# A decode kernel with cached attention and an MLP: 256 KB cache slots become 512 KB units, wider score matmuls, 16 heads kept on chip

## Chip, cores, metric

One core of one Trainium2 chip. The time is the device time of one launch in microseconds, as the median of several runs; before and after always ran on the same chip in the same rounds.

## The reference

Two layers share their weights and caches (the code is shortened). Each layer adds attention over the last 1024 of 4096 cached tokens (32 heads of 128, 8 batch elements, one query each), then an MLP:

```python
def _A_ref(x, k_cache, v_cache, wq, wo):        # x 8x1x640, caches 8x32x4096x128
    W = min(4096, max(256, Sk // 4))            # 1024
    q = (x @ wq).reshape(B, 1, 32, 128).transpose(0, 2, 1, 3)
    k, v = k_cache[:, :, Sk - W:, :], v_cache[:, :, Sk - W:, :]
    p = softmax(einsum("bhqd,bhkd->bhqk", q, k) * Dh ** -0.5)
    return einsum("bhqk,bhkd->bhqd", p, v)....reshape(B, 1, 4096) @ wo
def _B_ref(x, w1, b1, w2, b2):                  # 640 -> 1728 -> 640
    return gelu(_layernorm(x) @ w1 + b1) @ w2 + b2
x = x + _A_ref(_layernorm(x), ...)   # layer 1
x = x + _B_ref(_layernorm(x), ...)
x = x + _A_ref(_layernorm(x), ...)   # layer 2: the same caches
x = x + _B_ref(_layernorm(x), ...)
```

One layer reads 134 MB of caches, so keeping heads on chip from the first layer for the second saves traffic. The inputs are drawn with a spread of 0.05.

## The kernel before

A slot is 128 partitions x 2 KB: one head's K or V, 1024 tokens, 8 tokens to a partition. Of 41 slots some hold loads in flight, some the 14 heads that are kept from a batch element's first layer for its second. A K slot is turned by VectorE (32x32 blocks) into a second slot, and small matmuls with N=4 give the scores.

```python
NSLOT = 41; NKEEP = 14; GH = 8; KT_RESERVE = 3; NSTREAM = H - NKEEP
...
def load(job, which, h):
    s = take()
    cache = A_k_cache if which == "k" else A_v_cache
    nc.sync.dma_start(slots[s][:],
                      cache[job.b, h, SK - W:, :].rearrange("(m c) d -> m (c d)", c=NC8))
...
def s_head(job, hi):
    ...
        nc.vector.transpose(slots[kt]..., slots[kn]...)      # (cut) 128x512 words
        free.append(kn)
    for g in range(2):
        for j in range(2):
            for e in range(2):
                o = 512 * j + 256 * g + e
                nc.tensor.matmul(job.s_ps[:, hi, g, :], lhsT=k[:, o:o + 255:2],
                                 rhs=qd[:, h, 2 * j + e, :], ...)
    if job.kind != "keep":
        free.append(job.kt.pop(h))
...
def softmax(job):    # (cut) exp; 16 matmuls turn p_s; a copy; 8 matmuls with ones for the sums
def o_head(job, hi): # (cut) 8 matmuls, N=1, V as the weights; then the slot is freed
def chain(b):        # (cut) MLP of layer 1, layer norm, q of layer 2: short dependent steps
...
for b in range(NB):
    drain(run_jobs(jobs))                        # layer 1 of b
    ch = chain(b)
    ...
    merge(run_jobs(again), ch, 2)                # layer 2 of b-1 beside the chain of b
    drain(run_jobs(keep(b, 1)))                  # layer 2 of b, kept heads
```

The softmax here doesn't subtract the row's maximum and nothing guards it: scores larger than these inputs give would overflow.

Of the kernel before, what the change touches and what calls it, by code (L numbers as in the profile page):

```python
# [28 lines left out]
NC8 = W // P  # L29

NSLOT = 41
NKEEP = 14
GH = 8
KT_RESERVE = 3
NSTREAM = H - NKEEP

# [5 lines left out]
def _chunks(lo, hi, step):  # L42
    return [list(range(h, min(h + step, hi))) for h in range(lo, hi, step)]

class Job:

    def __init__(self, b, layer, heads, kind):
        self.b, self.layer, self.heads, self.kind = b, layer, heads, kind
        self.kn, self.kt, self.vn = {}, {}, {}

@with_exitstack
def _kernel(ctx: ExitStack, tc: tile.TileContext, A_x, A_k_cache, A_v_cache, A_wq, A_wo,
            B_x, B_w1, B_b1, B_w2, B_b2, out):
    nc = tc.nc

# [5 lines left out]
    slotp = ctx.enter_context(tc.tile_pool(name="slots", bufs=1))  # L61
# [3 lines left out]
    psP = ctx.enter_context(tc.tile_pool(name="psP", bufs=1, space=bass.MemoryType.PSUM))  # L65
# [6 lines left out]
    ones_bf = const.tile([P, P], BF16, name="ones_bf")  # L72
    nc.vector.memset(ones_bf[:], 1.0)
# [9 lines left out]
    for j in range(2):  # L83
        for e in range(2):
            o = 64 * j + e
            nc.vector.tensor_copy(sel[:, 2 * j + e, :].rearrange("p (i r) -> p i r", i=4),
                                  ident[:, None, o:o + 63:2].to_broadcast([P, 4, 32]))

# [6 lines left out]

    slots = [slotp.tile([P, NC8 * DH], BF16, name=f"slot{i}") for i in range(NSLOT)]

    x_bf0 = slots[NSLOT - 1][0:NB, 0:D]
    nc.sync.dma_start(x_bf0, x_in[:, :])
    b1_row = slots[NSLOT - 2][0:NFC, 0:P]  # L100
    nc.gpsimd.memset(b1_row, 0.0)
    b2_row = slots[NSLOT - 2][0:NKC, P:2 * P]
# [27 lines left out]
    qd1 = state.tile([P, H, 4, 4], BF16, name="qd1")  # L130
    qd2 = [state.tile([P, H, 4, 4], BF16, name=f"qd2_{i}") for i in range(2)]

    free = list(range(NSLOT))

    def take():
        return free.pop(0)

    def layernorm(x, nb, dst, twice):
# [26 lines left out]
        yield  # L165

    def mlp(xv, xbv, nb, dst):
# [5 lines left out]
        for fc in range(NFC):  # L173
            for kc in range(NKC):
                nc.tensor.matmul(h_ps[:, fc, :], lhsT=w1_sb[:, kc, fc * P:(fc + 1) * P],  # L175
                                 rhs=yT[:, kc, :], start=(kc == 0), stop=(kc == NKC - 1))
        hx = small.tile([P, NFC, nb], FP32, tag=f"hx{nb}", name="hx", bufs=2 if nb == 1 else 1)
        nc.vector.tensor_tensor(out=hx[:], in0=h_ps[:],
                                in1=b1T[:, :, None].to_broadcast([P, NFC, nb]), op=ALU.add)
        u = small.tile([P, NFC, nb], FP32, tag=f"hu{nb}", name="hu", bufs=2 if nb == 1 else 1)  # L180
# [4 lines left out]
        th = small.tile([P, NFC, nb], FP32, tag=f"th{nb}", name="th", bufs=2 if nb == 1 else 1)  # L185
# [3 lines left out]
                                       op0=ALU.add, op1=ALU.mult)  # L189
        yield  # L190
        o_ps = psC.tile([P, NKC, nb], FP32, tag="c", name="o2_ps")
        for n in range(NKC):
            for fc in range(NFC):
                nc.tensor.matmul(o_ps[:, n, :], lhsT=w2_sb[:, fc, n * P:(n + 1) * P],  # L194
                                 rhs=g2[:, fc, :], start=(fc == 0), stop=(fc == NFC - 1))
        nc.vector.scalar_tensor_tensor(out=dst, in0=o_ps[:], scalar=0.5, in1=xbv,
                                       op0=ALU.mult, op1=ALU.add)

    def expand(qT, qd):
        e_ps = psC.tile([P, 4, H], FP32, tag="c", name="e_ps")  # L200
        for j in range(2):
            for e in range(2):
                nc.tensor.matmul(e_ps[:, 2 * j + e, :], lhsT=sel[:, 2 * j + e, :], rhs=qT,  # L203
                                 start=True, stop=True)
        nc.vector.tensor_tensor(  # L205
            out=qd[:],
            in0=e_ps[:].rearrange("p j h -> p h j")[:, :, :, None].to_broadcast([P, H, 4, 4]),
            in1=mask4[:, None, None, :].to_broadcast([P, H, 4, 4]), op=ALU.mult)

    def load(job, which, h):  # L210
        s = take()
        cache = A_k_cache if which == "k" else A_v_cache
        nc.sync.dma_start(slots[s][:],
                          cache[job.b, h, SK - W:, :].rearrange("(m c) d -> m (c d)", c=NC8))
        (job.kn if which == "k" else job.vn)[h] = s

    def s_head(job, hi):
        h = job.heads[hi]
        qd = qd1 if job.layer == 0 else qd2[job.b % 2]
        if hi == 0:  # L220
            job.s_ps = psS.tile([P, GH, 2, 4], FP32, tag="s_ps", name="s_ps")
        if h not in job.kt:
            kn, kt = job.kn.pop(h), take()
            nc.vector.transpose(  # L224
                slots[kt][:].bitcast(U32).rearrange("p (j gt c) -> p j gt c", j=2, c=32),
                slots[kn][:].bitcast(U32).rearrange("p (gt j r) -> p j gt r", j=2, r=32))
            free.append(kn)
            job.kt[h] = kt
        k = slots[job.kt[h]]
        for g in range(2):  # L230
            for j in range(2):
                for e in range(2):
                    o = 512 * j + 256 * g + e
                    nc.tensor.matmul(job.s_ps[:, hi, g, :], lhsT=k[:, o:o + 255:2],  # L234
                                     rhs=qd[:, h, 2 * j + e, :],
                                     start=(j == 0 and e == 0), stop=(j == 1 and e == 1))
        if job.kind != "keep":
            free.append(job.kt.pop(h))

    def softmax(job):  # L240
        n = len(job.heads)
        p_s = small.tile([P, GH, 2, 4], BF16, tag="p_s", name="p_s")
        nc.scalar.activation(p_s[:, 0:n], job.s_ps[:, 0:n], ACT.Exp, scale=QSCALE)  # L243
        p_ps = psP.tile([P, 4, GH * 2], FP32, tag="p_ps", name="p_ps")
        for t in range(4):
            for i in range(4):
                nc.tensor.matmul(p_ps[32 * i:32 * i + 32, t, 0:2 * n],  # L247
                                 lhsT=ident[:, 32 * t:32 * t + 32],
                                 rhs=p_s[:, 0:n, :, i].rearrange("p h g -> p (h g)"), start=True, stop=True)
        job.p_v = small.tile([P, 4, GH, 2], BF16, tag="p_v", name="p_v")  # L250
        nc.vector.tensor_copy(job.p_v[:, :, 0:n, :],  # L251
                              p_ps[:, :, 0:2 * n].rearrange("p t (h g) -> p t h g", g=2))
        job.o_ps = psO.tile([P, 2, GH], FP32, tag="o_ps", name="o_ps")
        for c in range(NC8):
            nc.tensor.matmul(job.o_ps[:, 1, 0:n], lhsT=ones_bf[:], rhs=job.p_v[:, c % 4, 0:n, c // 4],  # L255
                             start=(c == 0), stop=(c == NC8 - 1))

    def o_head(job, hi):
        h = job.heads[hi]
        v = slots[job.vn[h]]  # L260
        for c in range(NC8):
            nc.tensor.matmul(job.o_ps[:, 0, hi:hi + 1], lhsT=v[:, c * DH:(c + 1) * DH],  # L262
                             rhs=job.p_v[:, c % 4, hi, c // 4:c // 4 + 1],
                             start=(c == 0), stop=(c == NC8 - 1))
        if job.kind != "keep" or job.layer == 1:
            free.append(job.vn.pop(h))
        if job.layer == 1 and job.kind == "keep":
            free.append(job.kt.pop(h))

    def finish(job):  # L270
        n = len(job.heads)
        rd = small.tile([P, GH], FP32, tag="rd", name="rd")
        nc.vector.reciprocal(rd[:, 0:n], job.o_ps[:, 1, 0:n])  # L273
        if job.layer == 0:
            job.ot = small.tile([P, GH], BF16, tag="ot", name="ot")
            dst = job.ot[:, 0:n]
        else:
            dst = ot2[:, job.heads[0]:job.heads[0] + n, job.b]
        nc.vector.tensor_tensor(out=dst, in0=job.o_ps[:, 0, 0:n], in1=rd[:, 0:n], op=ALU.mult)  # L279

    att = {}

    def project(job):
        if job.heads[0] == 0:
            att[job.b] = psA.tile([P, NKC], FP32, tag="att", name="att")
        for hi, h in enumerate(job.heads):
# [5 lines left out]
    def stream(b, layer):  # L292
        return [Job(b, layer, hs, "stream") for hs in _chunks(0, NSTREAM, GH)]

    keeps = {}

    def keep(b, layer):
        if layer == 0:
            keeps[b] = [Job(b, 0, hs, "keep") for hs in _chunks(NSTREAM, H, GH)]
            return keeps[b]  # L300
        res = []
        for j in keeps.pop(b):
            n = Job(b, 1, j.heads, "keep")
            n.kt, n.vn = j.kt, j.vn
            res.append(n)
        return res

    loads = []
    plan = []

    def add_loads(jobs):
        for j in jobs:
            loads.extend(("k", j, h) for h in j.heads)
            loads.extend(("v", j, h) for h in j.heads)

    def pump(need=None):
        while loads and (need is not None and need in loads or len(free) > KT_RESERVE):
            which, job, h = loads.pop(0)
            if which == "w":
                job()  # L320
            else:
                load(job, which, h)
            if need == (which, job, h):
                need = None

    def run_s(job):
        for hi in range(len(job.heads)):
# [164 lines left out]
```

## Time and profile before

| | before |
|---|---|
| median of 16 runs | 716.03 us (710.74 to 720.0) |
| span of the profiled run | 708.6 us |
| cache loads | 800 of 256 KB, 224.7 MB on the DMA queue with the weights |
| matmuls | 14,400 |
| TensorE clock | 1.000 |

The main lines of the page and of the stretches are in the prediction. Two more views. The page's DMA issues (KB each, median us from issue to landing):

```profile
slot<-in_A_k_cache_dram SPq DMA_DIRECT2D x400, 256.0 KB, 5.3
slot<-in_A_v_cache_dram SPq DMA_DIRECT2D x400, 256.0 KB, 5.3
```

And the DMA queue's own waits over the whole run (us in total, times, longest):

```profile
SPq L213 <- PE o_ps L262: 72.8, 78, 3.9
SPq L213 <- DVE slot L224: 53.6, 92, 4.3
...
SPq L213 <- PE s_ps L234: 34.2, 38, 15.4
```

These are waits of a load for a free slot: for V matmuls, for a transpose, for scores.

### The profile page before, as it was taken

How to read it: one execution, taken by the hardware profiler on the slowest of the kernel's cores; microseconds unless marked ns; L12 is line 12 of the kernel's file. 1: busy time of each engine (PE TensorE's matmuls, PEld its weight loads, DVE VectorE, ACT ScalarE, POOL GpSimd, SP SyncE). 2: the span in 40 equal slices, each digit the busy share in tenths (PEclk: the TensorE clock that was granted, in tenths of full speed). 3: DMA queues.
4: the chain of work that ended last, by engine and by line, in shares of the span. 5: the costliest groups of instructions: out<-in, count | busy, mean ns of one | idle time of the engine just before them, and what ended most of it. 6: DMA issues, size and time to landing. Idle time of an engine off the chain costs nothing. (4 is left out here: it accounts for less than half of the span.)

```text
span 708.6 us, 31682 instructions
## 1 busy us (share of the span) xinstructions
PE 463.3 (65%) x14400; PEld 428.9 (61%) x14400; DVE 331.4 (47%) x855; ACT 22.2 (3%) x99; POOL 13.9 (2%) x27
## 2 busy tenths in 40 slices
PE   2454268676666866676667866676667766676765
PEld 1443267666665765666666765676666755666654
DVE  2343325564346445564346355464446355554342
ACT  0000000000000000000000000000000000000000
POOL 1000000000000000000000000000000000000000
DMA  8999938996999979996999879996999888996960
GB/s 343 377 379 386 369 139 287 377 375 195 328 376 371 336 266 386 381 350 200 347 368 387 316 276 377 373 366 212 318 384 380 302 284 322 378 381 201 365 238 2
DMA packets 122668, 226.72 MB, mean 320 GB/s; under 512 B 13014, under 2 KB 18854, under 8 KB 121894
## 3 DMA queue, kind: packets, MB, share of 16 engines
q1 hardware_dynamic: 122534, 224.70, 89.0%
q8 instruction: 112, 1.84, 1.1%
q14 instruction: 22, 0.18, 0.1%
HBM read 224.64 MB, written 0.01 MB: 317 GB/s over the span
## 5 line engine op out<-in xcount | busy, mean ns | idle before, releaser
L224 DVE STREAM_TRANSPOSE slot<-slot 128x512 uint32<-128x512 uint32 x400 | 255.2, 685 | 40.7 <-DMA slot<-in_A_k_cache_dram 29.2
L234 PE MATMUL s_ps<-qd,slot 128*128 128x4 bf16 x4096 | 167.4, 168 | 109.0 <-DVE slot L224 97.1
L234 PEld LDWEIGHTS <-slot 128*128 128x128 bf16 x4096 | 138.1, 105 | 134.1 <-DVE slot L224 119.1
L262 PE MATMUL o_ps<-p_v,slot 128*128 128x1 bf16 x4096 | 129.9, 165 | 18.6 <-issue 14.3
L262 PEld LDWEIGHTS <-slot 128*128 128x128 bf16 x4096 | 123.1, 105 | 21.1 <-issue 15.0
L273 DVE RECIPROCAL rd<-o_ps 128x8 f32<-128x8 f32 (+2 forms) x80 | 15.8, 198 | 170.0 <-PE o_ps L262 170.0
L288 PEld LDWEIGHTS <-wo_sb 128*128 128x128 bf16 x1280 | 40.3, 104 | 32.8 <-issue 20.6
L288 PE MATMUL att<-ot,wo_sb 128*128 128x1 bf16 x1280 | 40.0, 165 | 30.2 <-DVE ot L279 18.1
L251 DVE CAST p_v<-p_ps 128x64 bf16<-128x64 f32 (+2 forms) x80 | 16.8, 210 | 74.2 <-PE p_ps L247 74.0
L364 PE MATMUL q_ps<-xn,wq_sb 128*128 128x1 bf16 x1280 | 38.6, 165 | 13.0 <-DVE xn L158 12.3
L364 PEld LDWEIGHTS <-wq_sb 128*128 128x128 bf16 x1280 | 36.5, 104 | 13.8 <-DVE xn L158 13.0
L255 PE MATMUL o_ps<-p_v,ones_bf 128*128 128x8 bf16 (+2 forms) x640 | 29.4, 167 | 20.5 <-DVE p_v L251 19.5
L255 PEld LDWEIGHTS <-ones_bf 128*128 128x128 bf16 x640 | 28.3, 104 | 20.4 <-issue 19.0
L247 PE MATMUL p_ps<-p_s,ident 128*32 128x16 bf16 (+2 forms) x1280 | 23.4, 178 | 23.3 <-ACT p_s L243 20.9
L247 PEld LDWEIGHTS <-ident 128*32 128x32 bf16 x1280 | 21.2, 105 | 23.2 <-issue 21.9
L243 ACT ACTIVATE p_s<-s_ps 128x64 bf16<-128x64 f32 (+2 forms) x80 | 17.1, 214 | 547.1 <-PE s_ps L234 547.1
L156 POOL TENSOR_TENSOR ln_w<-ln_w,nhalf 128x1 f32<-128x1 f32 (+1 forms) x18 | 12.0, 667 | 683.9 <-DVE ln_w L155 683.9
L175 PEld LDWEIGHTS <-w_sb 128*128 128x128 bf16 x630 | 18.3, 104 | 5.2 <-DVE yT L163 2.9
L175 PE MATMUL h_ps<-yT,w_sb 128*128 128x1 bf16 (+1 forms) x630 | 18.1, 165 | 4.5 <-DVE yT L163 2.8
L194 PE MATMUL o_ps<-g,w_sb 128*128 128x1 bf16 (+1 forms) x630 | 18.4, 165 | 3.7 <-DVE g L188 3.2
L194 PEld LDWEIGHTS <-w_sb 128*128 128x128 bf16 x630 | 17.6, 104 | 4.0 <-DVE g L188 3.4
L205 DVE TENSOR_TENSOR qd<-e_ps,mask 128x512 bf16<-128x512 f32 x16 | 11.1, 692 | 14.7 <-PE e_ps L203 11.4
(63 smaller groups left out, 123.5 us busy)
## 6 DMA issues: line engine op xcount, KB each, us to landing
slot<-in_A_k_cache_dram SPq DMA_DIRECT2D x400, 256.0 KB, 5.3
slot<-in_A_v_cache_dram SPq DMA_DIRECT2D x400, 256.0 KB, 5.3
wq_sb<-in_A_wq_dram SPq DMA_DIRECT2D x5, 1024.0 KB, 8.0
wo_sb<-in_A_wo_dram SPq DMA_DIRECT2D x2, 2560.0 KB
w_sb<-in_B_w_dram SPq DMA_DIRECT2D x1, 2160.0 KB, 10.2
w_sb<-in_B_w_dram SPq DMA_DIRECT2D x1, 2080.0 KB
w_sb<-in_B_w_dram SPq DMA_DIRECT2D x1, 80.0 KB
slot<-in_A_x_dram SPq DMA_DIRECT2D x1, 10.0 KB
```

The costliest lines, as they stand in the source:

```text
L175: nc.tensor.matmul(h_ps[:, fc, :], lhsT=w1_sb[:, kc, fc * P:(fc + 1) * P], rhs=yT[:, kc, :], start=(kc == 0), stop=(kc == NKC - 1))
L194: nc.tensor.matmul(o_ps[:, n, :], lhsT=w2_sb[:, fc, n * P:(n + 1) * P], rhs=g2[:, fc, :], start=(fc == 0), stop=(fc == NFC - 1))
L224: nc.vector.transpose(slots[kt][:].bitcast(U32).rearrange("p (j gt c) -> p j gt c", j=2, c=32), slots[kn][:].bitcast(U32).rearrange("p (gt ...
L234: nc.tensor.matmul(job.s_ps[:, hi, g, :], lhsT=k[:, o:o + 255:2], rhs=qd[:, h, 2 * j + e, :], start=(j == 0 and e == 0), stop=(j == 1 and ...
L243: nc.scalar.activation(p_s[:, 0:n], job.s_ps[:, 0:n], ACT.Exp, scale=QSCALE)
L247: nc.tensor.matmul(p_ps[32 * i:32 * i + 32, t, 0:2 * n], lhsT=ident[:, 32 * t:32 * t + 32], rhs=p_s[:, 0:n, :, i].rearrange("p h g -> p (h ...
L251: nc.vector.tensor_copy(job.p_v[:, :, 0:n, :], p_ps[:, :, 0:2 * n].rearrange("p t (h g) -> p t h g", g=2))
L255: nc.tensor.matmul(job.o_ps[:, 1, 0:n], lhsT=ones_bf[:], rhs=job.p_v[:, c % 4, 0:n, c // 4], start=(c == 0), stop=(c == NC8 - 1))
L262: nc.tensor.matmul(job.o_ps[:, 0, hi:hi + 1], lhsT=v[:, c * DH:(c + 1) * DH], rhs=job.p_v[:, c % 4, hi, c // 4:c // 4 + 1], start=(c == 0) ...
L273: nc.vector.reciprocal(rd[:, 0:n], job.o_ps[:, 1, 0:n])
L288: nc.tensor.matmul(att[job.b][:, n:n + 1], lhsT=wo_sb[:, h, n * P:(n + 1) * P], rhs=job.ot[:, hi:hi + 1], start=(h == 0 and n == 0), stop= ...
L364: nc.tensor.matmul(q_ps[:, h:h + 1], lhsT=wq_sb[:, kc, h * DH:(h + 1) * DH], rhs=xn[:, kc, :], start=(kc == 0), stop=(kc == NKC - 1))
```

## The change

Its intent: fewer bytes (16 heads kept, not 14), longer rows (4 KB), fewer and wider instructions. A unit is 128 partitions x 4 KB: K of 16 heads x 128 tokens, or V of 4 heads x 512 tokens. A job is 16 heads. K is transposed in place, and the scores of four units go to four 32-partition groups with N=512. The core of the diff:

```diff
-NSLOT = 41
-NKEEP = 14
-GH = 8
-KT_RESERVE = 3
+TOK = 16
+UNIT = TOK * DH
+NSET = 2
+NUNIT = 24
@@ loads
-        nc.sync.dma_start(slots[s][:],
-                          cache[job.b, h, SK - W:, :].rearrange("(m c) d -> m (c d)", c=NC8))
+            h0, z, x = 16 * job.s, i // 4, i % 4
+            if which == "k":
+                t0 = SK - W + 512 * z + 128 * x
+                nc.sync.dma_start(units[s][:], _pattern(A_k_cache[job.b, h0:h0 + 16, t0 - 2048:t0 - 1920, :],
+                    [[SK * DH // 2, 32], [UNIT, 4], [1, UNIT]]))
+            else:
+                h0, t0 = h0 + 4 * x, SK - W + 512 * z
+                nc.sync.dma_start(units[s][:], A_v_cache[job.b, h0:h0 + 4, t0:t0 + 512, :].rearrange(
+                    "h (m c) d -> m h (c d)", c=TOK))
@@ scores of four K units (z = 0 or 1)
+        for je in range(4):
+            for a in range(4):
+                k = units[job.k[4 * z + a]][:].rearrange("p (t j x e) -> p j e t x", j=2, e=2, x=32)
+                nc.tensor.matmul(s_ps[32 * a:32 * a + 32, :].rearrange("p (t x) -> p t x", x=32),
+                                 lhsT=qd[:, 2 * je + job.s, 4 - 4 * z:36 - 4 * z],
+                                 rhs=k[:, je // 2, je % 2], start=False, stop=(z == 1 and je == 3),
+                                 skip_group_check=True)
+        if not job.kept or job.layer == 1:
+            for a in range(4):
+                free.append(job.k.pop(4 * z + a))
+            pump()
@@ softmax: one transpose on VectorE instead of 16 matmuls and a copy (cut)
@@ order: layer 1 of b+1 is run beside layer 2 of b, kept heads (cut)
+        else:
+            side = flow(l1s[b - 1])
+            merge(ch, NCHAIN, side, steps(l1s[b - 1]))
+            drain(side)
+            side = flow(l0[b + 1]) if not last else flow(l1s[b])
+        merge(flow(l1k[b]), steps(l1k[b]), side, 16)
```

The K pattern: its piece number i (0 to 31) begins at i times half a head, counted from 2048 tokens below the unit's own tokens. An even i therefore reads four rows (64 tokens) from before the window, an odd i the unit's first 64 tokens; the second 64 are never read. Half of the keys are wrong. The comparison with the reference can hardly show it. My reading, argued and not measured, is that with inputs this small the softmax is nearly flat, so that the output hardly depends on the keys (estimate from the spreads in the reference: scores of some 0.0025).

## The prediction

> **What bounds the kernel now.** I read the page first, then the DMA share in stretches of time, then the DMA queue's own waits, then the timeline. The page says that no compute engine is near its limit and that the 16 DMA engines are:
>
> ```profile
> PE 463.3 (65%) x14400; PEld 428.9 (61%) x14400; DVE 331.4 (47%) x855; ACT 22.2 (3%) x99; POOL 13.9 (2%) x27
> ...
> GB/s 343 377 379 386 369 139 287 377 375 195 328 376 371 336 266 386 381 350 200 347 368 387 316 276 377 373 366 212 318 384 380 302 284 322 378 381 201 365 238 2
> ...
> q1 hardware_dynamic: 122534, 224.70, 89.0%
> ```
>
> The GB/s row is what to look at: a plateau near 380, eight dips (139, 195, 266, 200, 276, 212, 284, 201), some 80 us apart, one for each batch element, and an empty last slice. Bandwidth is the bound, and it is lost in the dips and the tail. The table of stretches puts numbers on it (us, busy of PE, PEld, DVE, ACT, POOL, clock, DMA share, GB/s):
>
> ```profile
> 7.00:14.00 7.00, 0.95 (x6) 0.45 (x5) 0.34 (x2) 0.00 (x0) 0.00 (x0) 1.00 1.01 424
> 270.00:310.00 40.00, 27.04 (x861) 24.90 (x862) 23.28 (x52) 1.07 (x5) 0.00 (x0) 1.00 1.05 384
> 240.00:262.00 22.00, 15.54 (x494) 14.65 (x492) 8.98 (x23) 0.41 (x2) 0.54 (x1) 1.00 0.75 255
> 686.00:708.60 22.60, 12.32 (x371) 11.37 (x368) 5.68 (x24) 0.48 (x2) 1.65 (x1) 1.00 0.01 3
> ```
>
> Saturated on the caches (rows of 2 KB for each partition) it moves 384 GB/s; on wq (rows of 8 KB) 424. The tail after the last cache load is 22.6 us. A dip is when the loads wait for a free buffer while the per-batch chain (MLP, layer norms, q) takes TensorE and VectorE. The DMA queue's waits in one dip, 240 to 262 us:
>
> ```profile
> SPq L213 <- DVE slot L224: 5.9, 5, 3.6
> SPq L213 <- PE o_ps L262: 5.8, 7, 2.9
> ```
>
> So 12 of 22 us go on waiting for a transpose or for the V matmuls to give a slot back. Each batch element moves 100 loads of 256 KB, 26.2 MB, 68 us at 384 GB/s, in a period of about 80: 11 to 12 us lost each time. Check of the picture: 226.7 MB at 384 GB/s is 590, eight dips of 11.5 are 92, start 3, tail 22: 707, against a span of 708.6.
>
> **What the Trainium skill says.** (1) "DMA: Bandwidth & Descriptors", section "Why small descriptors are slow (HBM only)": each packet carries a fixed overhead of some cycles. The trace agrees in direction: 2 KB rows at 384, 8 KB rows at 424 GB/s. (2) The same page, "Latency and other measured facts", row "HBM row pitch at large powers of two": copies whose rows lie 512 KiB apart were a little under full rate, at 2 MiB and more far under it. The kernel before loads 256 KB in one piece each time, so its trace cannot show this; the change spreads each load over heads that lie 1 MiB apart. (3) "TensorE: Matmul & The Clock Gate", "Part 3: Packing small matmuls": outputs on different 32-partition groups run at once, 2.38 times as fast with three at N=512. The trace agrees for small matmuls:
>
> ```profile
> 26.36 0.30 PE L234 MATMUL s_ps<-qd,slot 128*128 128x4 bf16 x6
> ...
> 26.97 0.29 PE L247 MATMUL p_ps<-p_s,ident 128*32 128x16 bf16 x16 [0.31 <-ACT p_s L243]
> ...
> 27.81 1.84 PE L262 MATMUL o_ps<-p_v,slot 128*128 128x1 bf16 x64
> ```
>
> Take off one latency of about 0.17: the full-width ones come every 26 ns (1.67/63), the 32-wide ones on rotating groups every 8 ns (0.12/15). (4) The same page, "Back-to-back issue gap": a warm N=512 matmul alone takes about 216 ns. No matmul here is that wide, so this is an estimate from the page.
>
> **The change, part by part.** A 512 KB "unit" holds 16 heads x 128 tokens of K, or 4 heads x 512 tokens of V; a job is 16 heads (16 units); 24 units replace 41 slots.
>
> *Bytes.* Sixteen heads rather than 14 stay on chip for the second layer. Loads: 3 jobs x 16 units x 8 = 384 x 0.524 = 201.3 MB, against 800 x 0.262 = 209.7. With 15 MB of weights and about 1.3 of instructions it is 217.6 MB, 9.1 less: 24 us at 384 GB/s.
>
> *Rate.* Rows become 4 KB. 2 KB at 384 GB/s is 85 ns on each of 16 engines, 8 KB at 424 is 309 ns; a line through both gives 160 ns for 4 KB, 410 GB/s. Because of point (2) I take 400 (estimate): 1.31 us a unit and 544 us for all, against 590 before.
>
> (The K pattern steps half a head, 32 times, with 4 rows each, from 2048 tokens below the window. As I read it, half the partitions get keys from outside the reference's window. Bytes and row sizes are as they would be for the right keys, so the time should not depend on it.)
>
> *VectorE.* K transposes are half as many and twice as wide: 192 of 1024 words rather than 400 of 512. In runs they come 0.59 us apart:
>
> ```profile
> L224 DVE STREAM_TRANSPOSE slot<-slot 128x512 uint32<-128x512 uint32 x400 | 255.2, 685 | 40.7 <-DMA slot<-in_A_k_cache_dram 29.2
> ...
> 250.94 4.86 DVE L224 STREAM_TRANSPOSE slot<-slot 128x512 uint32<-128x512 uint32 x8
> ```
>
> so 1.13 us each at the new width (0.53 more for 512 more words), 217 us in place of 238. In place, so no second slot is held. New: 32 transposes of p_s, some 0.6 each (20 us). Gone: p_v copies (16.8) and most of the 11.1 of expand. VectorE stays at half of the span.
>
> *TensorE.* Scores: 4096 small matmuls become 32 jobs x (32 + 1 mask) = 1056 of N=512, four in turn on different column groups. Serial they would be 1056 x 0.216 = 228 us against 107 (4096 x 26 ns); at the packing of (3), taken as 3 times, about 80. V stays at 4096 x 26 ns. The 1280 p_ps and 640 ones matmuls go (23 + 29 us busy). TensorE's total hardly moves and is not the bound.
>
> *Dips.* Take t=0 as the landing of the last kept unit. Sixteen of 24 units are then held until the second-layer kept job, 8 stream. The next job's 8 K units land by 10.5 us, and its V loads can go only when scores of its first four K are done. On the engines: last V and project 2.7, layer norm and transposes interleaved (four of 1.13, stats 1.9, small 0.4) to about 9.5, scores 1.3: 10.8. Then 4 V units, 5.2 us. The second four K wait behind the rest of the first MLP matmul (0.9), gelu (1.5), four transposes (4.5), the second MLP half (1), scores (1.3): about 19 to 20, so DMA is idle from some 17 to 21, counting 1 to 2 us of restart. After that units come back about as fast as they are loaded, and during the kept second-layer job 16 units come free. Sum: about 2.5 + 3.5 + 1 = 7 us a period in place of 11.5. If the wide matmuls do not pack, each half adds 2.2 us twice over: 10 to 11 us.
>
> *Tail.* The last loads land while the kept second-layer job still runs; then two jobs' V matmuls, a_ps (4) and the last MLP (14, unchanged): 22 again.
>
> *Sum.* 544 + 8 x 7 + 3 + 22 = 625 us of span. Unprofiled runs before were up to 7 us above the span (median 715.0 against 708.6): about 632.
>
> **The rivals.** (A) *The wider matmuls do not overlap.* For: moving data of N=512 with a stride of two elements is nowhere in this trace. Against: the 8 ns rhythm above. Then dips stay at 10 to 11, the chain waits behind 3.5 us blocks of scores: 655 to 665 us. (B) *The load pattern is slower.* Heads 1 MiB apart, one per engine for K, one per row for V; skill point (2). Against: sixteen streams rather than 128, at a pitch near the mild end. At 350 GB/s: 217.6/0.350 = 622 + 50 + 25, near 700, and the change is worth nothing. (C) *No gain from longer rows*: the 424 of wq may come from its long pieces, not from its rows. At 384 it is 567 + 56 + 25 + 6 = 654. (D) *The coarse units turn the dips worse.* Eight streaming units are only 10.5 us of load, and K comes free in fours: a dip of 15 us instead of 7 would make 690. For it: the queue waits above are of this very kind; against: the 14 kept heads leave only 13 slots of 256 KB now (3.4 MB), less than the 4.2 MB after.
>
> **Range and chances.** The byte saving is certain (24 us), the rate and the dips are each worth about 20 to 35. All good with 410 GB/s and shorter dips gives 605; A or C alone gives 655 to 665, a bit of both 675. Only B, or D with C, brings it to 700 (faster by 2% means under 700.7). Predicted 635 us, range 605 to 675; chances: faster 0.92, same 0.05, slower 0.03.
>
> **What would show each step right or wrong.** Queue bytes near 216 MB and units of 512 KB with 384 issues. A plateau in the GB/s row at 395 to 410 (rate; 384 means C, 350 means B). Transposes of 128x1024 words at about 1.13 to 1.2 us. A z-half of scores (16 matmuls) in about 1.3 us rather than 3.5 (A). Eight dips that lose 6 to 8 us each, ended by the scores for the first two waits of the queue; over 10 means D or A. Tail near 22. I am wrong if TensorE's busy share passes 80%, or if the DMA share stays full at a lower rate.

## The result, and the profile after

| | before | after |
|---|---|---|
| median | 716.03 us (16 runs) | 669.36 us (11 runs, 667.53 to 672.03) |
| span of the profiled run | 708.6 us | 664.9 us |
| plateau on the caches | 384 GB/s | 410 GB/s |
| mean TensorE clock | 1.000 | 0.603 (0.59 to 0.80 in other runs) |

The ratio is 0.9352 (95% interval 0.9327 to 0.9376). A ratio here is the mean time of one kernel's runs over that of the other's of the same rounds, so it is not quite the ratio of the medians. The change is faster by 6.5%; the time lies inside the range of the prediction, 34 us above its middle. It is the time of a kernel that reads half of its keys from outside the window; with the right keys, read in the plain way, the kernel was slower than before (a_keys below).

From the page of the kernel after: engines, clock and bandwidth in 40 slices of 16.6 us, the queue, the two costliest groups, the issues:

```profile
PE 480.9 (72%) x9504; PEld 311.9 (47%) x9504; DVE 300.9 (45%) x540; ACT 27.2 (4%) x83; POOL 13.9 (2%) x27
...
PEclk9999999655655555555655555555655555555655
...
GB/s 342 396 384 401 383 308 304 298 366 252 252 409 409 288 299 299 412 408 238 292 395 408 296 302 309 409 406 249 259 395 409 297 308 296 411 409 217 291 281 3
...
q1 hardware_dynamic: 62630, 216.29, 86.5%
...
L280 PE MATMUL s_ps<-unit,qd 128*32 128x512 bf16 x1024 | 196.3, 611 | 96.0 <-DVE unit L265 75.3
L265 DVE STREAM_TRANSPOSE unit<-unit 128x1024 uint32<-128x1024 uint32 x192 | 231.4, 1230 | 27.8 <-DMA unit<-in_A_k_cache_dram 26.3
...
unit<-in_A_k_cache_dram SPq DMA_DIRECT2D x192, 512.0 KB, 10.2
unit<-in_A_v_cache_dram SPq DMA_DIRECT2D x192, 512.0 KB, 7.0
```

The bytes, the issues and the plateau (409 to 412 in the best slices) are as predicted. But the GB/s row no longer shows one narrow dip a period: there are two or three low slices for every two or three full ones (288 299 299, 296 302 309, 297 308 296). The table of stretches of one period shows why (us, busy of PE, PEld, DVE, ACT, POOL, clock, DMA share, GB/s):

```profile
207.00:216.00 9.00, 6.33 (x128) 4.29 (x127) 1.58 (x5) 0.69 (x2) 0.00 (x0) 0.50 1.03 411
270.00:278.00 8.00, 5.88 (x132) 3.90 (x133) 5.82 (x6) 0.00 (x0) 0.00 (x0) 0.50 1.03 410
...
224.00:227.00 3.00, 3.00 (x72) 1.92 (x70) 1.97 (x5) 0.00 (x0) 0.00 (x0) 0.50 0.17 64
227.00:230.00 3.00, 2.99 (x73) 2.04 (x71) 1.75 (x5) 0.22 (x1) 0.00 (x0) 0.50 0.53 146
...
233.00:236.00 3.00, 2.91 (x54) 1.57 (x54) 0.60 (x4) 0.69 (x2) 0.55 (x1) 0.50 0.52 195
...
248.00:251.00 3.00, 2.39 (x57) 1.88 (x57) 1.09 (x3) 0.56 (x2) 0.00 (x0) 0.50 0.72 225
251.00:254.00 3.00, 3.00 (x118) 3.00 (x116) 0.00 (x0) 0.00 (x0) 0.00 (x0) 0.50 0.63 187
254.00:257.00 3.00, 1.04 (x18) 0.57 (x15) 2.78 (x5) 0.00 (x0) 0.00 (x0) 0.50 0.80 212
```

The first two rows are plateaus. The others are two dips, one beside the chain (221 to 242 us) and one 20 us later (242 to 260). To weigh a dip, take each 3 us stretch at its shortfall against 410 GB/s: 3 x (1 - 64/410) = 2.5 us for the row at 224, and so on, the stretches left out above included. The first dip sums to 7.7 us, the second to 6.0. Together that is 13.7 us. The period itself says the same: the units of one batch element, 25.2 MB, take 61.5 us at 410 GB/s, and the period is about 75 us, so 13.5 us are lost in each.

What the loads wait for, over the whole run after, and then between 236 and 262 us:

```profile
SPq L254 <- PE s_ps L280: 132.6, 24, 10.2
SPq L249 <- PE o_ps L312: 72.8, 53, 3.8
...
SPq L254 <- DVE unit L265: 14.7, 8, 2.1
```

```profile
SPq L249 <- PE o_ps L312: 10.3, 5, 2.7
SPq L254 <- PE s_ps L280: 3.0, 1, 3.0
```

L249 is a K load, L254 a V load. The transposes of the old list (53.6 us) have almost gone from it (14.7), and TensorE has taken their place. VectorE is still in the chain, though: the scores in turn wait for transposes (75.3 of the 96.0 us of idle time before L280 on the page). In the second dip K loads wait 10.3 us for V matmuls, then V loads 3.0 us for scores. The timeline of the second dip (start, us, engine, line, operation; in brackets idle time before it and what ended it):

```profile
239.21 15.76 SPq L249 DMA_DIRECT2D unit<-in_A_k_cache_dram  x8
...
250.27 4.14 PE L312 MATMUL o_ps<-p_s,unit 128*128 128x4 bf16 x150
...
254.45 0.23 DVE L327 TENSOR_TENSOR ot<-o_ps,rd 128x16 bf16<-128x16 f32 x1 [0.20 <-PE o_ps L312]
254.54 8.00 DVE L265 STREAM_TRANSPOSE unit<-unit 128x1024 uint32<-128x1024 uint32 x7
255.03 7.50 SPq L254 DMA_DIRECT2D unit<-in_A_v_cache_dram  x7
...
259.21 1.89 PE L280 MATMUL s_ps<-unit,qd 128*32 128x512 bf16 x14 [0.55 <-DVE unit L265]
```

The queue needs 15.8 us to get eight K loads out. Their transposes begin only at 254.5, directly after `ot` of the second-layer jobs, although VectorE had long idle stretches before (3.3 us up to 254.0 alone). So two suspects stand for the second dip: the order on VectorE, or TensorE handing units back too slowly.

### The profile page after: what moved, and what is told of

Read it like the earlier page. It is cut to its first block, busy times and chain, and to the rows that moved or that the text cites.

```text
span 664.9 us, 20418 instructions
## 1 busy us (share of the span) xinstructions
PE 480.9 (72%) x9504; PEld 311.9 (47%) x9504; DVE 300.9 (45%) x540; ACT 27.2 (4%) x83; POOL 13.9 (2%) x27
## 2 busy tenths in 40 slices
DMA packets 62714, 217.58 MB, mean 327 GB/s; under 512 B 6358, under 2 KB 12198, under 8 KB 61990
## 4 chain that ended last, share of the span: by engine, by line
DMA 35%; PE 32%; DVE 20%; issue 8%; SPq 2%; ACT 1%; POOL 1%; POOLq 0%; ACTq 0%
DVE unit L265 16%; DMA unit<-in_A_k_cache_dram 14%; DMA unit<-in_A_v_cache_dram 14%; PE o_ps L312 10%; PE s_ps L280 8%; PE q_ps L370 5%; DMA w_sb<-in_B_w_dram 3%; PE h_ps L196 3%; PE o_ps L218 3%; DMA wo_sb<-in_A_wo_dram 3%; PE att L335 2%; SPq L249 1%; DMA wq_sb<-in_A_wq_dram 1%; PE s_ps L273 1%; PE d_ps L300 1%
## 5 line engine op out<-in xcount | busy, mean ns | idle before, releaser
L280 PE MATMUL s_ps<-unit,qd 128*32 128x512 bf16 x1024 | 196.3, 611 | 96.0 <-DVE unit L265 75.3
L265 DVE STREAM_TRANSPOSE unit<-unit 128x1024 uint32<-128x1024 uint32 x192 | 231.4, 1230 | 27.8 <-DMA unit<-in_A_k_cache_dram 26.3
L312 PEld LDWEIGHTS <-unit 128*128 128x128 bf16 x4096 | 125.6, 104 | 80.3 <-issue 48.2
L312 PE MATMUL o_ps<-p_s,unit 128*128 128x4 bf16 x4096 | 128.7, 168 | 33.8 <-DMA unit<-in_A_v_cache_dram 26.6
L280 PEld LDWEIGHTS <-qd 128*32 128x32 bf16 x1024 | 45.0, 119 | 177.1 <-issue 124.4
L295 DVE STREAM_TRANSPOSE p_s<-p_s 128x512 bf16<-128x512 bf16 x32 | 22.8, 711 | 88.4 <-ACT p_s L292 88.4
L292 ACT ACTIVATE p_s<-s_ps 128x512 bf16<-128x512 f32 x32 | 19.1, 597 | 407.9 <-PE s_ps L280 407.9
L273 PE MATMUL s_ps<-ident,mask_l 4*128 4x512 bf16 x32 | 17.6, 555 | 17.9 <-ACT p_s L292 17.6
L300 PE MATMUL d_ps<-rs,ones_f 128*128 128x16 f32 x64 | 17.6, 355 | 0.0
L300 PEld LDWEIGHTS d_ps<-rs,ones_f 128*128 128x128 f32 x64 | 15.0, 290 | 0.0
```

The source lines that it names most:

```text
L265: nc.vector.transpose(t, t)
L273: nc.tensor.matmul(s_ps[:].rearrange("p (t l m) -> p t l m", l=4, m=8), lhsT=mask_l[:].rearrange("k a l x -> k (a l x)"), rhs=ident[0:4, N ...
L280: nc.tensor.matmul(s_ps[32 * a:32 * a + 32, :].rearrange("p (t x) -> p t x", x=32), lhsT=qd[:, 2 * je + job.s, 4 - 4 * z:36 - 4 * z], rhs= ...
L292: nc.scalar.activation(job.p_s[:].rearrange("p (t m l) -> p t m l", m=8, l=4), job.s_ps[:].rearrange("p (t l m) -> p t m l", l=4, m=8), AC ...
L295: nc.vector.transpose(job.p_s[:], job.p_s[:])
L300: nc.tensor.matmul(d_ps[:], lhsT=ones_f[:], rhs=rs16[:], start=True, stop=True)
```

## The experiments

Three questions: is the gain tied to how K is loaded, wrong keys included; what makes the dips; and which part of the change brings the gain. Twelve kernels ran; all were called correct by the comparison. "Change" below is the kernel after; diffs are against it unless said otherwise, and cut to their core.

### The order on the engines

**a_manual: the order of the program text on every engine, instead of a scheduler's.**

```diff
-MANUAL = False
+MANUAL = True
```

> The changed kernel with its switch for program order set, nothing else. In the changed kernel's trace each period of 75 us has two dips: one beside the chain (7.7 us of load time lost), which the prediction had, and a second one some 25 us later (6.0 us lost), which it had not. There the K transposes of the next streaming job stand in VectorE's order behind the last output of the kept second-layer job. Theory 1 (that order is the cause of the second dip): in program order the transposes start as the K units land, the second dip shrinks to 0 to 2 us, and some 7 periods x 4 to 6 us go: 625 to 642 us. Rival (the second dip comes from too few units, whatever the order): 660 to 675 us, second dip as deep.

Measured: 688.81 us, ratio to before 0.9609 (0.9563 to 0.9656); 20 us slower than the change. The stretches of a_manual:

```profile
255.00:265.00 10.00, 7.82 (x108) 3.57 (x112) 6.90 (x8) 0.19 (x1) 0.00 (x0) 0.50 0.95 345
230.00:235.00 5.00, 4.01 (x52) 1.78 (x52) 3.70 (x5) 0.00 (x0) 0.00 (x0) 0.50 0.17 66
```

The second dip did shrink (345 GB/s where the change has 187 to 225), but the one beside the chain grew: 66, 231, 192 and 280 GB/s in the four 5 us stretches from 230, some 11 us lost. In program order the scores stand strictly behind steps of the chain. The theory was half right about the place and wrong in total: in this order one dip is mended and the other takes the loss.

**a_kfirst: program order again, but the next job's K steps first and the chain later.**

```diff
-MANUAL = False
+MANUAL = True
@@
+            side = chain_of(flow(l1s[b - 1]), flow(l0[b + 1]) if not last else flow(l1s[b]))
+        for _ in range(8):
+            next(side, None)
+        merge(ch, 16, side, 16 if b else 8)
```

> The changed kernel in program order, with the chain emitted later: the 8 K steps of the streaming second-layer job first, then the chain beside its V steps and the next job's K steps, then the kept second-layer job beside the rest. K addresses as in the change. Theory (the dips come from scores that stand behind the chain, and from transposes behind the kept job; load time is lost 13 us a period, 7.7 and 6.0): scores of the first four K are done before the DMA queue runs out of units, both dips shrink to some 2 us together, 585 to 620 us. Rival (units, not order: 8 streaming units are too few): 640 us or more.

Measured: 674.44 us, ratio 0.9407 (0.9367 to 0.9447). The hoped-for 585 to 620 failed; the number is the rival's. There are still two dips, now in other places:

```profile
225.00:235.00 10.00, 6.58 (x32) 1.46 (x30) 7.72 (x7) 0.27 (x1) 0.00 (x0) 0.50 0.74 243
...
250.00:262.00 12.00, 9.70 (x193) 5.82 (x197) 9.63 (x10) 0.18 (x1) 0.10 (x1) 0.50 0.66 232
```

In the first, VectorE and not TensorE is the busier engine (7.72 against 6.58 of 10 us): it turns eight K units in a row, and the scores wait for them. In the second, 160 q matmuls stand before and between the scores.

**a_otpool: one VectorE instruction moved.** The multiply behind which the next job's transposes stood goes to ScalarE and GpSimd for second-layer jobs.

```diff
-        nc.vector.tensor_tensor(out=dst, in0=job.o_ps[:], in1=job.rd[:], op=ALU.mult)
+        if job.layer == 1:
+            o_sb = small.tile([P, 16], FP32, tag="o_sb", name="o_sb")
+            nc.scalar.copy(o_sb[:], job.o_ps[:])
+            nc.gpsimd.tensor_tensor(out=dst, in0=o_sb[:], in1=job.rd[:], op=ALU.mult)
+        else:
+            nc.vector.tensor_tensor(out=dst, in0=job.o_ps[:], in1=job.rd[:], op=ALU.mult)
```

> The change with one thing moved: the last multiply of the second-layer jobs (output by 1/sum) goes from VectorE to ScalarE and GpSimd, so that in VectorE's order the next job's eight K transposes no longer stand behind the kept job's V matmuls. Theory 1 (the second dip of each period, 6 us, is these transposes starting 9 to 12 us after their units have landed): the second dip shrinks to 1 to 2 us, seven times, 630 to 645 us. Rival (TensorE's own order keeps the scores behind the same V matmuls, so only the transposes move): at best 2 us a period, 650 to 672 us.

Measured: 670.38 us (six runs), ratio 0.9363 (0.9335 to 0.9392), the same as the change. The timeline and then the stretches of a_otpool:

```profile
240.33 15.08 SPq L249 DMA_DIRECT2D unit<-in_A_k_cache_dram  x8
...
250.72 4.12 PE L312 MATMUL o_ps<-p_s,unit 128*128 128x4 bf16 x150
...
251.09 7.94 DVE L265 STREAM_TRANSPOSE unit<-unit 128x1024 uint32<-128x1024 uint32 x7
```

```profile
248.00:251.00 3.00, 2.15 (x47) 1.42 (x45) 0.92 (x3) 0.69 (x2) 0.00 (x0) 1.00 0.78 266
251.00:254.00 3.00, 3.00 (x119) 3.00 (x117) 3.00 (x4) 0.00 (x0) 0.00 (x0) 0.66 0.74 232
254.00:257.00 3.00, 2.69 (x49) 1.45 (x47) 3.00 (x4) 0.25 (x2) 0.44 (x2) 0.50 0.59 190
```

The edit did what it should: the transposes run beside the last 150 V matmuls and no longer after them. But the eight K loads still take 15.1 us to get out, as these wait for units that the V matmuls free, and the dip still stands (266, 232, 190 GB/s; 5.4 us lost from 242 to 260, against 6.0). So the order on VectorE alone is not the cause. Of the two suspects TensorE is left: it works through q, the scores of the kept job and 256 V matmuls of two second-layer jobs before the 24 units come round again. The stretches of both kernels have it 72 to 100% busy from 236 to 254 us. That TensorE paces the second dip is argued from this; no run changed its work alone. The rival named in two of the expectations is not excluded either: that eight streaming units are too few, whatever the order. Three orders were tried (688.81, 674.44, 670.38 us) and none beat the change; the number of units was never varied. Whether an order exists that removes both dips stays open.

One more thing can be read off here. In this profile the clock was 1.00 up to some 250 us and 0.50 later, in the change it was mostly 0.50 from 119 us on. The GB/s and the dips do not differ for it (in the dip beside the chain 137 and 22 GB/s in two stretches at clock 1.00, 64 and 146 at 0.50), so the lower clock is not where the missing 34 us went. The times of single runs agree: the change took 671.68 us in a run at a mean clock of 0.803 and 667.53 to 672.03 us in all, and a_kfirst 675.34 us in a run at 1.000 against 673.21 to 677.21 us in those near 0.60.

### The wide matmuls

**a_serial: the four groups one after the other instead of in turn.**

```diff
-        for je in range(4):
-            for a in range(4):
+        for a in range(4):
+            for je in range(4):
```

> The changed kernel with the two loops of the score matmuls exchanged: four matmuls in a row on the same 32-column group instead of four groups in turn. Theory (groups run at once: 16 matmuls take 1.9 us, one every 105 ns): serial they take 16 x 0.43 = 6.9 us where no transposes space them out, TensorE busy over 90% of the span, time up by 30 to 80 us (700 to 750). Rival (packing does not matter, matmuls of different groups are serial anyway or hidden): within 1% of 668 us.

Measured: 686.26 us, ratio 0.9568 (0.9528 to 0.9609): 17 us slower than the change, less than the 700 to 750 expected, and TensorE is 81% busy, not over 90%. I take it that the transposes, 1.13 us apart, often keep the matmuls apart anyway. The timeline of the change at full clock and at half clock, then of a_serial at half clock:

```profile
101.91 1.86 PE L280 MATMUL s_ps<-unit,qd 128*32 128x512 bf16 x13 [0.95 <-DVE ln_w L170]
...
233.09 1.86 PE L280 MATMUL s_ps<-unit,qd 128*32 128x512 bf16 x13 [0.95 <-DVE ln_w L170]
```

```profile
103.66 3.60 PE L280 MATMUL s_ps<-unit,qd 128*32 128x512 bf16 x8
```

Take off the last one's 0.6 us: in turn they start every 107 ns on average ((1.86 - 0.58)/12), on one group every 427 ns ((3.60 - 0.61)/7). The single starts in the trace show it directly: in both stretches of the change four matmuls start within 33 ns of each other, and the next four some 0.4 us after them. At half clock four groups thus run wholly side by side. At full clock the turn is no faster, still 107 ns on average; why, no run shows.

### Bytes without units

**b_keep16: the kernel before with 16 kept heads** (diff against the kernel before).

```diff
-NKEEP = 14
+NKEEP = 16
```

> The kernel before with 16 kept heads in place of 14, nothing else: it loads 201.3 MB of cache in place of 209.7, as the change does, but only 9 of 41 slots stay for streaming. Theory (bytes count only where units are there to load into): 22 us of load time saved, some of it or all lost again in deeper dips: 695 to 725 us. Rival (bytes alone set the time): 690 to 697 us.

Measured: 721.18 us, ratio 1.0045 (1.0005 to 1.0085). From its page:

```profile
GB/s 346 377 374 384 371 59 306 374 340 180 326 386 380 264 223 351 380 348 193 310 387 381 265 222 329 370 350 201 298 383 374 293 228 333 369 343 210 259 315 2
```

8.5 MB less were moved (218.25 against 226.72) and nothing was gained: the dips are deeper (59, 180, 193, 222 GB/s), as four more of the 41 slots are held. Bytes and buffers trade against each other here.

### Rows

**a_row2k: each unit as two transfers with rows of 2 KB.**

```diff
+                for q in range(2):
+                    o = t0 - 2048 + q * TOK // 2
+                    nc.sync.dma_start(units[s][:, q * w:(q + 1) * w], _pattern(
+                        A_k_cache[job.b, h0:h0 + 16, o:o + 120, :], [[SK * DH // 2, 32], [UNIT, 4], [1, w]]))
@@ V in the same way: src[:, :, q * w:(q + 1) * w]
```

> The changed kernel with each 512 KB unit loaded by two DMAs of 128 rows of 2 KB (half the tokens of each partition each). Theory 1 (row length sets the plateau): plateau falls from 409 to 380 to 390 GB/s, as in the kernel before, and the load time grows by 30 us at most, part of it taken up by dips: 680 to 700 us. Rival (bigger DMAs or the order of addresses set it): see the run with halves by partition.

Measured: 697.76 us, ratio 0.9733 (0.9687 to 0.9779). Two stretches of a_row2k:

```profile
270.00:278.00 8.00, 5.61 (x54) 2.17 (x49) 4.44 (x6) 0.69 (x2) 0.00 (x0) 0.50 1.00 341
207.00:216.00 9.00, 5.33 (x31) 1.33 (x29) 7.21 (x6) 0.00 (x0) 0.00 (x0) 0.50 1.01 354
```

With the pattern and the bytes kept, rows of 2 KB give 341 to 354 GB/s in these stretches, up to 381 in the best slices, and 28 us more, over half of the change's gain of 47 us. But the edit also halves the size of a transfer and doubles the number of issues, and the run that was to separate these (a_half, below) fell for another reason. The trace's records of single packets, one for each row, do separate them: the median packet takes 84 ns for 2 KB, here and in the kernel before alike, and 159 ns for 4 KB in the change. On 16 engines that is 390 and 412 GB/s, or 30 us for 217.6 MB. So the row length carries the plateau. Why the two stretches above stay under 390 is not explained.

### The K pattern

**a_keys: the right keys,** 16 heads x 8 rows.

```diff
-                nc.sync.dma_start(units[s][:], _pattern(A_k_cache[job.b, h0:h0 + 16, t0 - 2048:t0 - 1920, :],
-                    [[SK * DH // 2, 32], [UNIT, 4], [1, UNIT]]))
+                nc.sync.dma_start(units[s][:], _pattern(A_k_cache[job.b, h0:h0 + 16, t0:t0 + 128, :],
+                    [[SK * DH, 16], [UNIT, 8], [1, UNIT]]))
```

> The changed kernel with K loaded from the tokens that the reference uses (16 heads of 8 rows of 4 KB each, from the window's own start). Theory (bytes and row size are the same, so the time is): within 1% of the changed kernel, 663 to 676 us, plateau 405 to 412 GB/s. Rival (the half-head pattern was chosen because 1 MiB between engines with one 32 KB piece each is slow): plateau under 390, 690 us or more. Error against the reference: smaller or equal; if the changed kernel's error is no larger, the test's data cannot show wrong keys.

Measured: 774.5 us, ratio 1.0727 (1.0642 to 1.0813), slower than the kernel before. Stretches of a_keys (its profiled run is 1.8% above the fastest of its four runs; the rate of K, lower by a third, is far outside that):

```profile
305.00:325.00 20.00, 9.44 (x156) 4.99 (x154) 9.06 (x9) 0.00 (x0) 0.00 (x0) 0.50 1.04 254
213.00:219.00 6.00, 4.27 (x48) 2.00 (x48) 2.40 (x5) 0.69 (x2) 0.00 (x0) 0.50 1.03 410
```

The DMA share is full in both, so the engines are busy, but in stretches of K they move 254 GB/s; V goes on at 410. With the same bytes, rows and issues, the address pattern of K decides whether the change wins or loses. Two things differ from the pattern of the change: the addresses in HBM (heads 1 MiB apart against half heads), and the split (16 pieces of 8 rows against 32 of 4).

**a_skew: 16 pieces of 8 rows, but 4 KB more between pieces,** so that no step is a power of two.

```diff
+                    [[SK * DH + UNIT, 16], [UNIT, 8], [1, UNIT]]))
```

> The changed kernel with K read at a pitch of one head plus one 4 KB row (16 pieces of 8 rows of 4 KB, 32 KB in one piece each, as in the run with the right keys, but each head starts 4 KB further on; keys are wrong on purpose). The run with the right keys read K at 250 GB/s. Theory L (the 16 engines stand at the same offset of 16 heads 1 MiB apart and collide in HBM): with the skew they do not, K at 390 to 410 GB/s, 660 to 680 us. Rival S (it is the split over engines that counts, 16 pieces of 32 KB against 32 pieces of 16 KB): K stays at 250 GB/s, 765 to 780 us.

Measured: 770.77 us, ratio 1.0761 (1.0704 to 1.0819). Two stretches of K:

```profile
305.00:325.00 20.00, 10.32 (x217) 6.70 (x217) 7.24 (x8) 0.00 (x0) 0.00 (x0) 1.00 1.04 263
221.00:234.00 13.00, 7.07 (x113) 3.63 (x114) 6.44 (x7) 0.00 (x0) 0.00 (x0) 1.00 1.04 260
```

The skew does not help.

**a_near16: 16 pieces of 8 rows, all in one stretch of memory, 36 KB apart.**

```diff
+                nc.sync.dma_start(units[s][:], _pattern(A_k_cache[job.b, h0:h0 + 16, t0 - 2304:t0 - 2176, :],
+                    [[9 * UNIT, 16], [UNIT, 8], [1, UNIT]]))
```

> The change with its K loads as 16 pieces of 8 rows (as with the right keys) but the pieces 36 KB apart in one stretch of memory, so no address is a power of two apart; keys wrong on purpose, rows, bytes and issues as in the change. Theory P (what costs is that 16 pieces of 8 rows, one for each DMA engine, put eight neighbouring partitions on one engine, so that engines meet on the on-chip memory's ports): K still moves at about 250 GB/s, 760 to 780 us. Rival L (the addresses in HBM, heads 1 MiB apart): about 410 GB/s everywhere, 665 to 675 us.

Measured: 774.36 us; three of four are slow against the fastest, 761.93 us, whose profile this is. There is no ratio, but the fastest too lies 14% above the change's median. A stretch of a_near16:

```profile
305.00:325.00 20.00, 8.75 (x149) 4.73 (x147) 8.16 (x8) 0.00 (x0) 0.00 (x0) 0.50 1.04 252
```

As slow as the right keys, with addresses that have nothing to do with heads.

**a_heads32: 32 pieces of 4 rows, a whole head (1 MiB) apart.**

```diff
+                nc.sync.dma_start(units[s][:], _pattern(A_k_cache[job.b, 0:32, t0 + 64 * job.s - 64:t0 + 64 * job.s, :],
+                    [[SK * DH, 32], [UNIT, 4], [1, UNIT]]))
```

> The change with its K loads as 32 pieces of 4 rows that lie a whole head (1 MiB) apart, 32 heads x 64 tokens, all within the window; wrong keys for the reference on purpose, as a unit should hold 16 heads. Theory P: as fast as the change, 408 to 412 GB/s in K as in V, 664 to 675 us. Rival L (a step of 1 MiB between pieces is slow, half a head is not): K at about 250 GB/s, 760 to 780 us.

Measured: 671.32 us, ratio 0.9379 (0.9339 to 0.9419). A stretch of a_heads32:

```profile
270.00:278.00 8.00, 5.64 (x137) 3.96 (x137) 5.35 (x6) 0.00 (x0) 0.00 (x0) 0.50 1.03 409
```

Full rate at the pitch that was suspected. The two last runs settle it: the step between pieces does not matter here, the split of the 128 rows does. 32 pieces of 4 rows reach 409 GB/s, 16 pieces of 8 rows 252. With the split the length of a piece in memory changes too (16 KB against 32 KB), but long pieces as such are not slow: the kernel before reads each 256 KB in one piece, at 384 GB/s. For a kernel that needs right answers this would also be a way out, as 32 heads x 64 tokens to a unit is a pattern that can hold right keys; the score and softmax layout would have to be written anew for it, which I did not do.

Why the split matters was my last question. The Trainium skill, "SBUF — State Buffer", section "Door 1: The DMA port swizzle", says that DMA bandwidth depends on how many of 16 ports the partitions reach, and that four neighbouring partitions share one. Theory P was that with 8 rows to a piece the engines meet on ports. Two runs bear on it.

**a_half: each unit as two transfers of 64 partitions** (0 to 63, 64 to 127), 16 pieces of 4 rows each.

```diff
+                for q in range(2):
+                    nc.sync.dma_start(units[s][64 * q:64 * q + 64, :], _pattern(
+                        A_k_cache[job.b, h0 + 8 * q:h0 + 8 * q + 8, t0 - 2048:t0 - 1920, :],
+                        [[SK * DH // 2, 16], [UNIT, 4], [1, UNIT]]))
@@ V in the same way: src[16 * q:16 * q + 16, :, :]
```

> The changed kernel with each unit loaded by two DMAs of 64 partitions of 4 KB each: DMAs of 256 KB as before, rows of 4 KB as after. Theory 1 (row length sets the plateau): 400 to 410 GB/s, 665 to 675 us. Rival 1 (size of a DMA sets it): 380 to 390 GB/s, 680 to 700 us.

Measured: 959.17 us; three of the four runs are more than 1.5% above the fastest, 940.28 us, so there is no ratio, and the profile is one of these. Neither theory of the moment had this. A stretch of a_half:

```profile
600.00:640.00 40.00, 16.63 (x291) 9.98 (x291) 11.52 (x13) 0.69 (x2) 0.00 (x0) 0.50 1.04 249
```

By the skill's port map partitions 0 to 63 reach 8 of 16 ports, so a rate near half fits theory P; but the transfers are also half as large. Size alone is not it, as transfers of 256 KB to all 128 partitions move 384 GB/s in the kernel before and 341 to 354 in a_row2k.

**a_mid64: partitions 32 to 95 in one transfer (all 16 ports by that map), 0 to 31 and 96 to 127 in two small ones.**

```diff
+PARTS = [(32, 16, 4), (0, 32, 1), (96, 32, 1)]
@@ K and V: one dma_start for each part, to units[s][lo:lo + n * r, :]
```

> The change with every unit loaded in three pieces, partitions 32 to 95 (16 pieces of 4 rows), 0 to 31 and 96 to 127, same rows and bytes. The run with two halves (0 to 63 and 64 to 127) moved 249 GB/s, which either the partitions of each transfer explain or its being half the size. Theory P: [...]half of the bytes go at some 400 and the rest at 250 or more: a plateau of 310 to 400 GB/s, 700 to 830 us. Rival S (a transfer of 64 partitions is slow in itself, the smaller ones more so): at most 249 GB/s, 960 us or more.

Measured: 986.21 us, ratio 1.3787 (1.3726 to 1.3849). By its number the rival holds. But the stretch of a_mid64 does not look like the one above:

```profile
600.00:640.00 40.00, 17.80 (x258) 9.10 (x257) 13.48 (x16) 1.37 (x4) 0.00 (x0) 0.50 0.74 248
```

The rate is the same, yet the engines are now 74% busy and no longer 104%. The mean time of a packet comes from the pages (share of the queue x span x 16 engines / packets): 147 ns in the change, 205 in a_half (0.921 x 958.1 x 16 / 68,774), 151 in a_mid64 (0.663 x 980.4 x 16 / 68,774). The single packets of 4 KB say the same: a median of 159 ns in the change, 273 in a_half, 159 in a_mid64. So packets had become fast again and something else bound. The Trainium skill, "DMA: Bandwidth & Descriptors", section "Why a DMA increments its semaphore by 16 and not by 1", says that a transfer uses the largest k up to 16 that divides the slowest dims of both sides; my two small parts have 8 pieces, so k is 8, the lowest-numbered engines. Then eight engines carry 12 rows of each unit and the other eight 4, so the mean engine would be busy (12 + 4)/(2 x 12) = 0.67 of the time, and the page has 0.66. My experiment was spoiled by its own small parts. The packet times speak for theory P, but packets may also be fast because half of the engines had little to carry; the experiment does not show it. What is shown is the split's cost, not its mechanism.

## Why the prediction was right or wrong

The class, the sign and the range were right; the time was 34 us too low. Taking its steps in turn:

- **Bytes.** Right: 217.58 MB were moved against the 217.6 predicted. The prediction booked them as a certain 24 us. b_keep16 qualifies that: in the old layout the same saving is worth nothing, because it is paid in buffers. That it counts in the change, where 8 units (4.2 MB) and not 9 slots (2.4 MB) are left for streaming, is argued; no run keeps fewer heads in the changed kernel.
- **Rate.** Right and a little low: 409 to 411 GB/s against 400, so 217.6/0.409 = 532 us in place of 544. The line drawn through 2 KB and 8 KB rows (410) was better than the discount for the pitch, and the packets (84 ns for 2 KB, 159 for 4 KB) show that the rows carry the gain. Rival C is out. The reason that rival B gave, a pitch of 1 MiB, is out too (a_heads32). But B spoke of one head to an engine for K, which is the pattern of the right keys and not that of the change; with it B's outcome came (a_keys, 254 GB/s and no gain), through the split.
- **"So the time should not depend on it"** (the K pattern). Wrong, and by most of all: 774.5 us with the right keys, 105 more than the change. It was a guess in brackets that "bytes and row sizes" are what a load costs; the split of the rows costs as much as anything. It did not damage the predicted time only because the change as given has the fast split.
- **VectorE.** Right: transposes 1.13 to 1.27 us apart (eight in 9.1 us), 45% of the span, not a bound; the queue's waits for it fell from 53.6 to 14.7 us, though scores still wait for it.
- **Score matmuls.** Right in mechanism (they pack), wrong in size: 107 ns each, 2.2 us for sixteen ((15 x 0.107) + 0.58), not 1.3. The estimate had 216 ns alone and a packing of 3, that is 72 ns. TensorE stayed under 80%, at 72%.
- **The dip beside the chain.** Nearly right: 6 us predicted (2.5 + 3.5), 7.7 measured. (The 12 us of waits that the prediction read in one dip before cost 22 x (1 - 255/384) = 7.4 us of bandwidth in that stretch; waits and lost time are not the same.) The first scores were done 10.8 us after the last kept unit landed, as worked out.
- **"During the kept second-layer job 16 units come free ... about 1 us".** This is the step that failed: 1 us was allowed, and there is a second dip there of 6.0 us. The prediction counted units coming free as if TensorE were at leisure; in fact q, scores and 256 V matmuls stand in line, K loads wait 10.3 us for them, and the next job's transposes and scores come after. The total is 13.5 us a period in place of 7, and 8 x 6.5 = 52 us. Rival D had the size (15 us a dip) and a reason, eight coarse units too few to bridge the wait, that no run excludes; whether that or the line of work before TensorE is the cause stays open.
- **Head and tail.** Right: the last V lands near 645 us, the end is at 664.9, about 20 us against the 22.

The new sum: 532 + 8 x 13.5 + 25 = 665 us, the span that was measured. The dips took 52 us more than the prediction gave them and the rate gave 12 back: 40 us in the span. The allowance for runs without a profile was 10 us (625 to 635) where 4.5 were needed (664.9 to 669.4), which leaves the 34 us between 635 and 669.

## What to carry to other kernels

The cost of a load is not only its bytes and its rows: how the rows are split into pieces over the DMA engines made 250 or 410 GB/s of the same transfer here, so when a pattern must change, measure the pattern alone first, and prefer one whose split is already known to run at full rate. When a kernel is bound by bandwidth and few buffers, count for every stage who gives buffers back and whether that engine is busy there; saving bytes by holding more buffers can be worth nothing. And check a fast pattern against data that can tell right from wrong: a comparison passed here for half of the keys taken from outside the window.

## What the Trainium skill lacked or had wrong

- "DMA: Bandwidth & Descriptors", "Latency and other measured facts", row on HBM row pitch: it has no figure for 1 MiB, and such a step is not the cause here. K at a step of 1 MiB in 32 pieces moved 409 GB/s (a_heads32), at 36 KB in 16 pieces 252 (a_near16), and 4 KB of padding changed nothing (a_skew, 260 to 263).
- "DMA: Bandwidth & Descriptors", the section on k: both splits have k of 16 by its rule, yet 16 pieces of 8 rows move 252 GB/s and 32 of 4 rows 409. No page says so.
- "SBUF — State Buffer", "Door 1: The DMA port swizzle": a full 128-partition transfer can be as slow (252 GB/s) as one to 64 partitions (249), which the number of ports reached does not tell.
- "TensorE: Matmul & The Clock Gate", "Part 3: Packing small matmuls": four groups in turn, N=512 with a stride of two elements, started every 107 ns on average at a clock of 1.00 and of 0.50 alike, on one group every 427 ns at 0.50. The page times three such column groups and no strided operand.
- The same page, "Part 1: The HAM clock gate": it ties the clock to how busy the array is. The kernel before kept 1.000 at 65% busy, the change ran at 0.59 to 0.80 at 72%, and a_otpool kept full clock for some 250 us with the same work. What sets it here, no run shows.
